# A third buffer for a rational MLP's polynomial, and a new order of work, behind gated linear attention

## The chip, the cores and the metric

The kernel runs on one core of a Trainium2 chip (trn2). The metric is device time in microseconds of one execution; kernels are compared by the median of several runs.

## What is computed

Gated linear attention over 4 batches of 8 heads, 768 tokens, head dimension 48, and behind it an MLP with a rational function in place of an activation. In the reference's words, cut:

```python
for t in range(S):
    state = alpha[:, :, t, :, None] * state + einsum('bhd,bhe->bhde', k[:, :, t], v[:, :, t])
    y[:, :, t] = einsum('bhd,bhde->bhe', q[:, :, t], state)
x = y.transpose(0, 2, 1, 3).reshape(3072, 384)
h = x @ w_in                               # 384 -> 2048
P = a[0] + a[1] * h + a[2] * h**2 + a[3] * h**3
Q = 1.0 + abs(b[0]) * abs(h) + abs(b[1]) * h**2
out = (P / (Q + 1e-06)) @ w_out            # 2048 -> 384
```

The inputs q, k, v and alpha are float32; the weights and coefficients come as float64.

## The kernel before

**Attention.** The sequence is cut in chunks of 128 tokens, and products of alpha are made with scans on VectorE (`suffix`, `prefix`), for 24 groups n of two chunks and four heads each. GpSimd multiplies k and q by them. 48 pieces i (a chunk and four heads) then go through TensorE (`sc_mm`), ScalarE (`sc_evac`), GpSimd (`sc_mask`, `decay`), TensorE again (`attn_mm`) and VectorE (`kv_add`). Two pieces make a chunk's output in PSUM bank 3, which ScalarE and VectorE split into a high and a low part (`x_hi`, `x_lo`), x for the MLP.

**Weights.** They come as pairs of 32-bit words of float64. Each of the 16 blocks (first layer i, second layer o, j = 0 to 7) is made float32 by one ScalarE step and three VectorE steps (`join_abs`, `join_sign`, `join_low`, `join`) and then split into a high part (ScalarE, `split_hi`) and a low part (`split_lo`; VectorE for j below 4, GpSimd from there).

**MLP.** There are 96 units u: 12 blocks of 256 tokens by 8 slices of 256 hidden columns. The first two token blocks are taken in two phases (slices 0 to 5, then 6 and 7), so that work can start before all weights are there. A unit's first layer (`mlp_in`, L562) is 18 products into PSUM bank u % 3; its second layer is 8 products with the high part gh (`mlp_out_hi`, L623) and 4 with the low part gl (`mlp_out_lo`, L633). Between them, on a 128 x 512 tile each:

- ScalarE: `act_t1` (L572) makes a2 + a3 h in tile t1; `act_ah` (L569) makes |h| in ah; `act_q1` (L575) makes b0 + b1 |h| in qm
- GpSimd: `pool_qm` (L578) multiplies qm by ah
- VectorE: `dve_t2`, `dve_t3` (L582, L586) go on with the polynomial in t1
- ScalarE: `act_ars`, `act_sq` (L589, L592) make a first reciprocal of Q in the PSUM bank
- VectorE: `dve_p`, `dve_t`, `dve_g` (L596, L599, L605) improve it and leave the quotient in t1
- ScalarE: `act_gh` (L608) makes gh from t1; GpSimd (VectorE for the first eight units): `sub_gl` (L612) makes gl from t1 and gh

So t1 holds the polynomial and then the quotient, and is free only when gl is done. t1, ah and qm have two buffers each, gh three, gl two. The bank is free for unit u + 3 when `dve_g` of unit u is done. The names in the profile leave buffer numbers out: t stands for t1.

**The verdict.** The fast attention is good for alpha within bounds. 18 loads of alpha and 36 ScalarE steps (`guard`, L663) count what is outside. After all other work `guard_verdict` sums this (VectorE, L672), adds over partitions (TensorE, L673, into bank 3) and compares with zero (VectorE, L675). Every engine then loads the result `ok` (L937) and branches on it (L938); a general path stands behind the branch, and does not run here.

**The order.** Every step is given to a `Plan` with its engine and the steps that it comes after. `Plan.run` issues the steps in the order of `ORDER`, a compressed list of numbers that was searched ahead of time. Each engine takes its own steps in that order, and waits on semaphores where a step needs another engine's result.

Of the kernel before, what the change touches and what calls it, by code (L numbers as in the profile page):

```python
# [12 lines left out]
F32 = mybir.dt.float32  # L13
# [9 lines left out]
class Plan:  # L23
# [35 lines left out]
    '6#q~Ml~o<b-;_vYQ(q{pnu5FO1d94gd+0n~!ka3mQu-gA#R~}fhDxVUUst5R(k+!<X?+p1tIOC=Wl-f*ke-TH(5T{y',
    'bwJ%!k@Q{?ZPgvMkG_#tMn6`;`a1=w`zo@w`UkyN<yDAw`kC_jfePpf>Ygg7DyoO7kgB8}sa&eC`k=z}b5%rrRG~Ut',  # L60
    '-&QZwQ&m|-(dY1+imIdOcj}F*ql&5@>WR96arGyaTgB5JqU%>Gy^f*d>+gz{R(VuRok4$933P<ctLm!Hs)S0Y>!~2f',
    'q)V!d`mM^W>#G1H)>(7|C6HAo(TTK!Z2F5TrIPAoT0=fnS|!&FRb+^zv+EQ(wyvryq||YA4qZkCLqXk2<<tzRbRk_$',
    'rPh%kjV`RKD+6hD5nV$S)#-Fq{ZiFb)$}h_OXboDpt>%uYwEa=TfbI~RSDf($A_P)n9ieH=n#kvC3Rk%PiKNZs+7Kp',
    'HFPX!qFU<wy0-qS;=nZ|D4_qT(z=$8fI9j*meKK`u5PMsVr!iN>S+ZTp}uaT(?bJYRs%HDJ#{(VOf}NIbYtCImDi(n',
    'Z~a@fP_6VBoe28swz`jQrxOA~1>Ik_*A;bQ7^?^9dss<#&`F@Rx{V!mKV4Z@(Vg@iY@*w!rh1_6tncD@-As4UZPi>o',
    'NO#rkR5v|XPtfD^JUv8rR1<Z3)m_imLv;_mP*2k9btp{Mi}WqLkHd6kND5Q*aNR>q)emtRmVlmWfgYi!=_mLIv%&_w',
    'SWnlFF$;{;8}$-BO3%<mp_f{!59<dwQ)h!^`iS1Fm+NBi5?AP1dW$})i^EDiTW`{<^c>w=9oK90R=ryHQET-!-B+#C',
    '$8;EM*C%xj*r8A9TyR2P)jM@|*rl)O(>fe-!gal$Zs-FP1<vT*IyyYXTl%ctqo3h9eOsT`&vBpLtCPcieL+WsWKb5~',
    '=offXmxcp68oa_Xa7cGj2X$xlRv)D4SOE@E4EU$t={vd<e9&FgYb+0U^+nxPDJ}_l;GPEVrt$)EBe<{M>&Eavzrlz4',
    'qrRk@L4S2wKhkfpDSXmb^kc1gfO?1JV4#Y|O&|qC=Y}vyHGmlWS*L_2da$YwsUSCe(W#*>5P#KmV2Jvr>%n*ZLq~90',  # L70
    'c&cA{;h*}sf2IxBhF|)*t_aEbg=X#yG5MALtz&aXNCTGt=s5gRJN~O<aTj>$J%7Lezt-s>E~ns55EI^G5dXlBm=AJt',
    'N{+<2_!Fk)$Q+M@IXB1W5KhAhI2DI-Le9&du@HoDB96je@i5K6w49j3xilZ4Zy1%+@psI_N%#w<=cJsU|6xAPz{$7(',
    'XXKxl9}03NE&_%4H)iGnP?)oD8UBMsI4fu4Us#qaL3S?Bf3Ya%;O<b4D{y6~%f+}GROC0lIM?G!+#4!$2`&g-p+2|g',
    'D%=B@8gNxE$%UaOG~{YrieLD~+=%-?2X4Z>Kv8vW%2l8SBX#7N*c@u|QF`l%YVk1|0ks*Z6KiS#!=Vm0;~LPF2Xbc~',
    '2hI7l@4|z)1&@SoEL0W7!eDO6wID#<xf-;DQP7Gfa}RFK6JRL!<TgAJdU0DG#zVL_x8u<;oTqRf9s?t|FR$WhJRU~!',
    'RPM*sVLE^C{dp3M;#pi1R`U!V&0}~bTUx`jc^wbnu{?*@v!Olgs4vXrz3gc&jN^G6O7ma>&*yzSo+t7GKEMkgh!*le',
    'UdxmCIL*QhyolfV`LLKz&_-Uu`?(b?<xL!!R`4Ni4a>M4tmMPIna}ZZ4yG-9o{#WW4xvbNl(%shMW+jVj61+~zQo5l',
    '3hm%FaDt=KP7bHb{D3cVKRC%(cnL(KUHsl(<%fKV7eRlx#=H3uFN3ylnjiBDxXx$z8ONa~e3ox;d-&`>`Ni;wZ}L-q',
    '&L919_{_KX1%LAcAO_v$mpmEna0Gqf+4zdL!Z&`+cX=QTfv>y;?(rLrML+mHf9HkpmIuL4W;sclAvXQuQzR0Tw!v?H',
    '$5Y@v8~MXK-~$f>D~aeYe`F`yAt2G^tN+Jdc0rIRi6J{-Dnt?xl$f#)NFvK%h$Xv0ON0bV3W+Uy;ENBDl(HA%$WZw1',  # L80
    'LnW2OrJp{v#FeEGCet83#gq7wU*b`?B%lNmMG{IvN+VGvk))Lr6iw1gVo4_jB!jGkq%s{cN)nj?ry-dXluS}lPC_Bc',
    'EVCfF6qYlPMJmZ}UsQ_7Daa~`sj?K4Igm|eLUBn-bFhSDm&THWl2J)HO--bfB&RBJhSE|FDJ@N9HsqA*QbwvuE~z19',
    'Wj}P4+>%!wK{aV6-K4p+lm}2wYDz0<A$g>{)ROy9L265Dc?c<~j<k`w(p~aNDrzhBWVrN{c2ZwfLuzUu?d1yek{;4f',
    'RzU}8Bp0E#q@iEFlk}1E&{0N6U%3D?rJt;UQF0kN%Sh=jYvCMpkqt0f2FNTq3qSlo86#t5kgS$VFk8mSU>PDRunxw{',
    'A3s#q!vq;7b7YN7lua;KHo_!HM{8xCOqTUBU((ZDoFWTkgY1>Fv{25`R5<|CWRYZ`>GBvB%M4j3OC%#bg?;kZZ<J@S',
    'N%l)7Iv`8s32c@ubO@Ho71<)0X}KJdt+GP0(l%KshvlGbmsPSuj>uKXMi@9MJ7t#~gln=}j>%Pc1&86f?2$Zl1ir#?',
    'c_z2y1RR4Kazb9fbNS~_%1!wWw<SBhkW+F;a?(+lhp*&0{E)kngI>#d`T_UkwEUF&l8au#8M#1b<(E8=Z*Wd>(@S{`',
    '=Y;|f<v6^NNEk4e<gHwgM-q&W<()i{KN1<A%5V8ALHJ(s(m&zAMfo6w=(6M|9r!591epTl0-pp-LCQyQ%xAd<Xuil-',
# [44 lines left out]
NNAT = 2  # L133
WB = 2
GB = 3
NSC = 2
TB = 2


@with_exitstack  # L140
def tile_gla_then_rational_mlp(ctx, tc, q, k, v, alpha, w_in, w_out, ca, cb, out):
    nc = tc.nc
    B, H, S, D = q.shape
    DM = H * D
# [381 lines left out]
    XB = 2  # L526
# [443 lines left out]
```

## Time and profile before

| | us |
|---|---|
| median of 3 runs | 604.32 |
| lowest and highest run | 602.88, 605.81 |
| the profiled execution, its own time | 600.71 |
| its span, first to last instruction | 599.0 |
| mean granted TensorE clock | 0.97 |

The span's rows are of one profiled execution. Busy time counts instructions that do work; loads of registers, branches and semaphores do not count. "PEld" is TensorE's loading of weights, which overlaps its products. A q behind an engine's name (SPq, PEldq) is its sequencer. An idle time is put down to the instruction that released the waiting one.

### The profile page before, as it was taken

To read this page: it belongs to the slowest core of one execution; us is meant where nothing else is said; L and a number is where in the kernel's file an instruction comes from. 1 tells how busy PE (TensorE), PEld (TensorE's weight loads), DVE (VectorE), ACT (ScalarE), POOL (GpSimd) and SP (SyncE) were. 2 spreads that over 40 slices of the span, in tenths; PEclk is the share of its full clock that TensorE was granted. 3 is DMA by queue.
4 is the path that set the end of the run, shared out by engine and by line. 5 is a ranking of instruction groups with operands and counts; after the bars stand their busy time and mean duration, and the time that the engine had idled before them with its cause. 6 is when DMAs were issued, how large, how long until landed. Compare 5 with 4: busy or idle time off the path is not lost. (4 is left out here: it accounts for less than half of the span.)

```text
span 599.0 us, 14096 instructions
## 1 busy us (share of the span) xinstructions
PE 540.2 (90%) x5362; PEld 503.4 (84%) x5362; DVE 503.8 (84%) x782; ACT 475.5 (79%) x803; POOL 400.3 (67%) x422
## 2 busy tenths in 40 slices
PE   4958359798789999999999999999999999999994
PEld 2647248697689999999999999999999999999993
DVE  4489999899979989989979889889889798778773
ACT  4478467687768799989898999998888787887972
POOL 6675453657687767687676777677766767565562
PEclk9998779799989999999999999999999999999999
DMA  9998542212442443414244344425230000000000
GB/s 170 248 367 275 94 55 32 30 28 34 56 94 58 72 80 72 64 28 69 61 68 89 49 92 79 76 47 76 30 44 26 14 27 2 2 27 1 27 1 32
DMA packets 179979, 41.90 MB, mean 70 GB/s; under 512 B 169409, under 2 KB 172481, under 8 KB 179905
## 3 DMA queue, kind: packets, MB, share of 16 engines
q1 hardware_dynamic: 179904, 40.94, 34.9%
q8 instruction: 44, 0.72, 0.5%
q14 instruction: 31, 0.25, 0.1%
HBM read 36.18 MB, written 4.72 MB: 68 GB/s over the span
## 5 line engine op out<-in xcount | busy, mean ns | idle before, releaser
L562 PE MATMUL ps<-x,wi 128*128 128x256 f32 x1728 | 232.7, 287 | 16.2 <-ACT wi L250 7.4
L562 PEld LDWEIGHTS ps<-x,wi 128*128 128x128 f32 x1728 | 220.9, 192 | 26.4 <-ACT wi L250 7.8
L623 PE MATMUL ps<-wo,gh 128*128 128x384 f32 x768 | 157.6, 344 | 16.2 <-DVE wo L257 6.7
L578 POOL TENSOR_TENSOR qm<-qm,ah 128x512 f32<-128x512 f32 x96 | 128.0, 1336 | 50.4 <-ACT qm L575 49.2
L612 POOL TENSOR_TENSOR gl<-t,gh 128x512 fp32r<-128x512 f32 x88 | 117.6, 1338 | 61.6 <-issue 30.3
L623 PEld LDWEIGHTS ps<-wo,gh 128*128 128x128 f32 x768 | 132.3, 190 | 21.3 <-DVE wo L257 6.9
L582 DVE TENSOR_TENSOR t<-t,ps 128x512 f32<-128x512 f32 x96 | 65.2, 680 | 33.6 <-ACT t L572 32.0
L633 PE MATMUL ps<-wo,gl 128*128 128x384 f32 x384 | 84.4, 342 | 0.3 <-POOL gl L612 0.3
L596 DVE SCALAR_TENSOR_TENSOR t<-t,coef,ps 128x512 f32<-128x512 f32 x96 | 71.0, 739 | 16.1 <-ACT ps L592 15.6
L575 ACT ACTIVATE qm<-ah,bab 128x512 f32<-128x512 f32 x96 | 77.8, 810 | 5.6 <-DVE ps L599 4.4
L589 ACT ACTIVATE ps<-qm,one_eps 128x512 f32<-128x512 f32 x96 | 66.1, 688 | 19.9 <-POOL qm L578 9.8
L572 ACT ACTIVATE t<-ps,coef 128x512 f32<-128x512 f32 x96 | 74.3, 774 | 7.3 <-POOL gl L612 4.3
L569 ACT ACTIVATE ah<-ps 128x512 f32<-128x512 f32 x96 | 56.9, 593 | 27.9 <-PE ps L562 26.5
L586 DVE SCALAR_TENSOR_TENSOR t<-t,coef,ps 128x512 f32<-128x512 f32 x96 | 71.4, 745 | 3.8 <-ACT ah L569 1.3
L608 ACT ACTIVATE gh<-t 128x512 fp32r<-128x512 f32 x96 | 60.1, 626 | 18.1 <-DVE t L605 16.0
L633 PEld LDWEIGHTS ps<-wo,gl 128*128 128x128 f32 x384 | 68.9, 191 | 1.4 <-POOL gl L612 0.9
L605 DVE SCALAR_TENSOR_TENSOR t<-ps,t 128x512 f32<-128x512 f32 x96 | 65.9, 687 | 2.1
L599 DVE SCALAR_TENSOR_TENSOR ps<-qm,ps 128x512 f32<-128x512 f32 x96 | 65.9, 687 | 0.0
L592 ACT ACTIVATE ps<-ps 128x512 f32<-128x512 f32 x96 | 56.1, 584 | 1.7
L444 PE MATMUL ps<-tq,tk 48*128 48x192 f32 (+1 forms) x384 | 46.1, 360 | 4.6 <-POOL tk L415 3.0
L457 POOL TENSOR_SCALAR_AFFINE_SELECT sc<-sc 128x512 f32<-128x512 f32 x48 | 31.9, 666 | 20.3 <-ACT sc L453 19.8
L453 ACT ACTIVATE sc<-ps 128x768 f32<-128x768 f32 (+1 forms) x48 | 37.0, 771 | 6.0 <-PE ps L444 3.6
(94 smaller groups left out, 603.9 us busy)
## 6 DMA issues: line engine op xcount, KB each, us to landing
wi_words<-in_moe_w_in_dram SPq DMA_DIRECT2D x8, 768.0 KB, 8.9
wo_words<-in_moe_w_out_dram SPq DMA_DIRECT2D x8, 768.0 KB, 10.3
tv<-in_v_dram SPq DMA_DIRECT2D x24, 192.0 KB, 3.2
wr<-in_alpha_dram SPq DMA_DIRECT2D x18, 256.0 KB, 2.9
out_dram<-parts SPq DMA_DIRECT2D x24, 192.0 KB, 2.0
raw_a<-in_alpha_dram SPq DMA_DIRECT2D x80, 32.0 KB, 2.1
raw_k<-in_k_dram SPq DMA_DIRECT2D x80, 32.0 KB, 2.1
raw_q<-in_q_dram SPq DMA_DIRECT2D x80, 32.0 KB, 2.1
```

Source lines behind the costliest of these rows:

```text
L562: nc.tensor.matmul(h_of(u)[:, ff * SEG : (ff + 1) * SEG], split_w["i", j][:, kt * FU + ff, w, :], x[:, kt, xp, :], start=(kt == 0 and n == ...
L572: nc.scalar.activation(buf(s, "t1", u), h_of(u), AF.Identity, bias=a2, scale=a3)
L575: nc.scalar.activation(buf(s, "qm", u), buf(s, "ah", u), AF.Identity, bias=b0, scale=b1)
L578: nc.gpsimd.tensor_tensor(buf(s, "qm", u), buf(s, "qm", u), buf(s, "ah", u), op=ALU.mult)
L586: nc.vector.scalar_tensor_tensor(t, t, a1, h_of(u), op0=ALU.add, op1=ALU.mult)
L589: nc.scalar.activation(h_of(u), buf(s, "qm", u), AF.Abs_reciprocal_sqrt, bias=one_eps)
L596: nc.vector.scalar_tensor_tensor(t, t, a0, h_of(u), op0=ALU.add, op1=ALU.mult)
L599: nc.vector.scalar_tensor_tensor(h_of(u), buf(s, "qm", u), 1.0 + 1e-6, h_of(u), op0=ALU.add, op1=ALU.mult)
L605: nc.vector.scalar_tensor_tensor(t, h_of(u), 2.0, t, op0=ALU.subtract, op1=ALU.mult)
L612: (nc.vector if GL_DVE[0] <= u < GL_DVE[1] and s is fast_bufs else nc.gpsimd).tensor_tensor(buf(s, "gl", u).rearrange("p a b -> p (a b)"), ...
L623: nc.tensor.matmul(o_of(tt), buf(s, "gh", u)[:, ff, tt * P : (tt + 1) * P], split_w["o", j][:, ff, w, :], start=(j == j0 and ff == 0 and w ...
L633: nc.tensor.matmul(o_of(tt), buf(s, "gl", u)[:, ff, tt * P : (tt + 1) * P], split_w["o", j][:, ff, 0, :], start=False, stop=(j == j1 and f ...
```

## The change

Three things change. The ring of t1 gets a third buffer (`TB`), so that `act_t1` of unit u waits for gl and gh of unit u - 3 in place of u - 2; the buffer counts of ah, qm and x get names, with the same values as before. The verdict's three instructions and its memset become steps of the plan. And `ORDER` is another list, so that steps of all engines stand elsewhere.

```diff
 ORDER = [
...
-    (the old list, 2846 steps)
+    (the new list, 2850 steps)
...
-TB = 2
+TB = 3
+QB = 2
+AB = 2
+NXB = 2
...
-    XB = 2
+    XB = NXB
...
-        "ah": ring("ah", 2, [P, N]), "t1": ring("t1", TB, [P, N]), "qm": ring("qm", 2, [P, N]),
+        "ah": ring("ah", AB, [P, N]), "t1": ring("t1", TB, [P, N]), "qm": ring("qm", QB, [P, N]),
...
-    def guard_verdict():
-        ones = const.tile([P, 1], F32, name="ones")
-        nc.gpsimd.memset(ones, 1.0)
-        tot = const.tile([P, 1], F32, name="tot")
-        nc.vector.tensor_reduce(tot, beyond, op=ALU.add, axis=mybir.AxisListType.X)
-        nc.tensor.matmul(ps[0:1, 3 * BANK : 3 * BANK + 1], tot, ones, start=True, stop=True)
-        ok = const.tile([1, 1], I32, name="ok")
+    vd_ones = const.tile([P, 1], F32, name="ones")
+    vd_tot = const.tile([P, 1], F32, name="tot_beyond")
+    ok = const.tile([1, 1], I32, name="ok")
+
+    def verdict_sum():
+        nc.vector.tensor_reduce(vd_tot, beyond, op=ALU.add, axis=mybir.AxisListType.X)
+
+    def verdict_mm():
+        nc.tensor.matmul(ps[0:1, 3 * BANK : 3 * BANK + 1], vd_tot, vd_ones, start=True, stop=True)
+
+    def verdict_ok():
         nc.vector.tensor_scalar(ok, ps[0:1, 3 * BANK : 3 * BANK + 1], 0.0, None, op0=ALU.is_equal)
-        return ok
...
-        add(("ah", u), "ACT", 0.6, act_ah, (u, fb), ins + [("qm", u - 2)])
+        add(("ah", u), "ACT", 0.6, act_ah, (u, fb), ins + [("qm", u - AB)])
...
-        add(("q1", u), "ACT", 0.82, act_q1, (u, fb), [("ah", u), ("t", u - 2), "bab"])
+        add(("q1", u), "ACT", 0.82, act_q1, (u, fb), [("ah", u), ("t", u - QB), "bab"])
...
+    add("vd_ones", "POOL", 0.1, nc.gpsimd.memset, (vd_ones, 1.0))
+    add("vd_sum", "DVE", 0.2, verdict_sum, (), [("gu", n, j) for n in range(NG) for j in range(2)])
+    add("vd_mm", "PE", 0.3, verdict_mm, (), ["vd_sum", "vd_ones", ("xl", 2 * NBLK - 1)], lat=0.13)
+    add("vd_ok", "DVE", 0.15, verdict_ok, (), ["vd_mm"], due=T0 + PACE * (NUA - 4))
...
-    ok = guard_verdict()
```

A list decodes with base85, zlib and 16-bit numbers; number n is the n-th step that the program adds to the plan. An engine's own order is what is left when the steps of the others are taken out. TensorE's last steps, as decoded ("in" a first layer, "out" a second layer, both by unit, "ol" the low part of a second layer; in 94 stands between the halves of out 90's high part):

```
before: in 89, in 90, out 86, out 87, in 91, in 92, out 88, out 89, in 93, in 94 (within out 90), out 90, out 91, in 95, out 92, out 93, out 94, out 95
after:  in 89, out 85, in 90, out 86, in 91, out 87, in 92, out 88, in 93, out 89, in 94 (within out 90), out 90, in 95, out 91, out 92, out 93, out 94, out 95
```

And VectorE around the verdict's steps and the last x_lo, as decoded:

```
after: ... p 82, t 82, g 82, x_lo 23, t2 83, ...    ... t2 87, t3 87, comparison of the verdict, p 86, t 86, ...
TensorE after: ... out 79, in 85, product of the verdict, out 80, out 81, ...
```

## Rows read from the trace of the kernel before

**Rows 1.** busy us and instructions by stretch: PE, PEld, DVE, ACT, POOL; clock; DMA; GB/s

```profile
0.00:36.00 36.00, 24.07 (x254) 17.95 (x255) 19.65 (x30) 17.49 (x37) 24.23 (x52) 1.00 1.14 230
...
36.00:165.00 129.00, 94.60 (x908) 84.85 (x906) 120.31 (x174) 90.92 (x138) 75.09 (x73) 0.88 0.45 97
...
200.00:540.00 340.00, 339.42 (x3553) 322.46 (x3552) 295.05 (x472) 298.79 (x517) 245.22 (x248) 1.00 0.29 52
...
540.00:593.00 53.00, 48.87 (x326) 46.86 (x324) 38.36 (x59) 41.35 (x69) 28.21 (x23) 1.00 0.02 9
```

**Rows 2.** waits, engine and line waited for: us, times, longest us, TensorE, whole span

```profile
PE ps L562 <- ACT wi L250: 7.4, 1, 7.4
...
PE ps L623 <- DVE wo L257: 6.7, 1, 6.7
```

**Rows 3.** timeline of the end: start, us, instruction, idle before it

```profile
578.05 0.68 DVE L605 SCALAR_TENSOR_TENSOR t<-ps,t 128x512 f32<-128x512 f32 x1
...
578.79 2.39 PE L562 MATMUL ps<-x,wi 128*128 128x256 f32 x18 [0.99 <-DVE t L605]
...
587.76 1.69 PE L623 MATMUL ps<-wo,gh 128*128 128x384 f32 x8 [2.34 <-ACT gh L608]
...
592.18 0.19 PE L673 MATMUL ps<-ones,tot 128*1 128x1 f32 x2
...
592.29 0.87 ACT L645 ACTIVATE parts<-ps 128x384 f32<-128x384 f32 x2 [2.54 <-PE ps L633]
```

**Rows 4.** chain that ended last, 515 to 540 us: start, us, what

```profile
524.91 4.26 PE ps L562 x36
...
529.17 1.39 PE ps L623 x8
...
533.86 0.70 PE ps L633 x4
```

**Rows 5.** groups by line, ScalarE's six: busy us, mean ns | idle before

```profile
L572 ACT ACTIVATE t<-ps,coef 128x512 f32<-128x512 f32 x96 | 74.3, 774 | 7.3 <-POOL gl L612 4.3 <-PE ps L562 2.3 <-DVE gl L612 0.3
...
L575 ACT ACTIVATE qm<-ah,bab 128x512 f32<-128x512 f32 x96 | 77.8, 810 | 5.6 <-DVE ps L599 4.4
...
L589 ACT ACTIVATE ps<-qm,one_eps 128x512 f32<-128x512 f32 x96 | 66.1, 688 | 19.9 <-POOL qm L578 9.8 <-DVE t L586 8.1 <-POOL tot L406 0.7
...
L608 ACT ACTIVATE gh<-t 128x512 fp32r<-128x512 f32 x96 | 60.1, 626 | 18.1 <-DVE t L605 16.0 <-DVE tot L672 1.4
...
L569 ACT ACTIVATE ah<-ps 128x512 f32<-128x512 f32 x96 | 56.9, 593 | 27.9 <-PE ps L562 26.5 <-DVE t L582 0.8
...
L592 ACT ACTIVATE ps<-ps 128x512 f32<-128x512 f32 x96 | 56.1, 584 | 1.7
```

**Rows 6.** instructions of L938 and L648 at the end, ns min/median/max

```profile
L938 ACTq COMPARE_BRANCH  x1: 50/50/50, 593.1 to 593.1; - x1
...
L938 PEldq COMPARE_BRANCH  x1: 3744/3744/3744, 593.2 to 593.2; - x1
...
L938 SPq EVENT_SEMAPHORE  x8: 17/17/17, 597.1 to 597.6; - x8
...
DMA to landing us min/median/max: 1.8/2.7/3.6
```

**Rows 7.** groups by line, four of VectorE's steps

```profile
L401 DVE TENSOR_TENSOR_SCAN fp<-ta,d 128x516 f32<-128x516 f32 x24 | 35.1, 1460 | 0.2
...
L537 DVE TENSOR_TENSOR x<-ps,x 128x384 fp32r<-128x384 f32 x24 | 13.1, 545 | 2.1 <-ACT x L532 2.1
...
L586 DVE SCALAR_TENSOR_TENSOR t<-t,coef,ps 128x512 f32<-128x512 f32 x96 | 71.4, 745 | 3.8 <-ACT ah L569 1.3
...
L380 DVE STREAM_TRANSPOSE tk<-raw_k 128x512 f32<-128x512 f32 x20 | 13.8, 691 | 0.0
```

**Rows 8.** instructions of L235 and L257 by form, ns min/median/max

```profile
L235 DVE SCALAR_TENSOR_TENSOR wi_words<-wi_words x8: 932/950/2020, 7.3 to 133.3; 128x768 uint32<-128x768 uint32 x8
...
L257 POOL TENSOR_TENSOR wi<-wr,wi x4: 1828/2200/3561, 66.9 to 139.1; 128x768 fp32r<-128x768 f32 x4
```

More of the change, by code (lines that the diff above doesn't have):

```diff
@@ L59 @@
[L59 to L88, printed above, removed]
@@ new lines @@
+    'U4?yA8{Vnc>KGlSG>{1L!x2gfIpHWJgO-pMl0$b$2Pq&Iq=%Hy2r|G=RRA(WaVQACR6oc9x#5q>3LW6L0==L9D%5Y(',
+    'LCOZ%;W)ilAJifGr^-PjeS)UYN3~m>p~#x_Cv}PTD5V9?(`OZ=E!+dGPf`?ZAez2F55WWLQ*@DTKy)3fPm|F%;fpE{',
+    'XG!#Z_^K+vJGe}R-~;ScS177JM|a_y+NZv&!Vp8>f*&eGSA^?O1f0$TURQ!UP!#gQBM8-%A%T7mF?E=J47VX4)PeNc',
+    'pw;0zgO1R3L1PI>r~|qlJb+9(u}-9`0^<|NsOy8r%(^5r0E<a<7VR*WPO7WHTZpYoK{6dz3qFI=5Kjj%xo!wkDTU6e',
+    'Q|jkXP`83N@B&^!DqTpY)>U<39Y+_{)gitvqO0jLPy^EF8al1cri<z7x+bL4we?fDLD_XJsG}oe4qaRaVNU%Ta_Pnp',
+    '2}|gjItn&{k~+7prAz6b&|Ei#x;h@V(Dn2mh>Ll2OPx>G*RLQx=GUcl9Q+Gq^i@(AfPYX{x7PRQ3pCI@bvfNeU!zaZ',
@@ new lines @@
+    'Q1{Y}bb0*|n!#w@M}LOAx;c!|fUR@^-CMWSEnuwfulwp>&`w{caIBy^!T?=SBevIJ7!@n&4mtu`!%eEJJL*VKMYn;k',
+    '&_p-ZKcJ~@3*&S%{T({#e!3k@)Zbvd?yTFxK%D?5>A8B44#q6lMbFcN^#t7mGT?9MrswOPkPy4;$$E$;oT3xqP`yz1',
+    'g7rEv4%1!r2Au?Z!vftyXU4^Pk?sSxX{yeI8+Biprti=QogQz|NWEE4*I99iKCEZxyA%zV>Wny3AJIv1na+jF^?iCm',
+    '$8-r?p@-|EdZm6y#qqd4ski8>`Vl>#oOnvF(vRty&W@XOCm5xR;td@guj^TQzsiQQ^#Qe7Z`E^j4&0{K=oolYzocRq',
+    'f=_9??hMmthkizP^a;IFKc}^NmyU_+^l80Y-_kEAIlj?*bSRd?Gy1KrfM@kyy-&Z>=X6=zuVdkReO@2X<?*h*p#SMZ',
+    '`jft`Kj>r#d{N)ipLIz@enkiMecc60A@OTUfnA{tzM<0iKz9Sh5A}39s2*v}Z|RV_q#tX;q1+!nYT=kX0KVvycv%mG',
@@ new lines @@
+    'uR0cA(XlZVrp9+P2)^mGI2gX`A@D=T;oO*<f9i@@7oX@9oEK|j9(<~qV{<cnrsMH*od)Zp<@lVEU+9MD_?P}bue9gR',
+    '_>q3=xE$a=Iu+N!_Y{f$>Q9t_({dNg$&vX7rQ=4Jnxk+o4&x>m&Ow}p^KeIu;Lnts^K&{(&rOj*LxR9pO2~ORA2!C)',
+    '{Ea%{VfBT|@OLV}i8uovQ4KI32Xk4@$Wgf-X5z$LkbhD%o<Zd~2EWw*C^MJi*ZMbA;O9OISLC`Jo&V4;3gN6=i3{;7',
+    'UymzuVg5@=xCl4kLYS0`a(zz5jky@-$I94{+jDU)fK|8&_r?zV!dK-++zYF5HtxiIupnmVrksO&Vl%GJg|P&8<mOz1',
+    '2XYJU%r&_y58~Ip8+YN7JcL_vDXxUAxCpYE%-wl7cgNP;gGcZb?tz23ClBRXTm`$~bgs=^u@?{HX<UbU^9%-6184C_',
+    'p3Qxj)J&SmM^$s2%58WQA5%(=#I{@uQB}n`yoyJ&R>QFx&gJUZj^FrExSC)3c^pt9uqMuDqt@_SzkomZzHHSPUdUtF',
@@ new lines @@
+    'seUYK53l8x=+!#jz>{z<M^)o^Bd_O)c#d1(K0d&$a5P3zn|K`d#e=+=qp0I*9&X{*c%FmQ2{oR_U}V*w+u#M>%E4*^',
+    '4&eQ~jW6*8UVw*q5kKJVe3-}LWxmJ{c|0EBD;!fz<fA-`u5vq^#PjhOU*pBx7U$x1Uc!%fDc|57e4L}H6}*hw<4Qik',
+    'k9j%AP&fG`cfecxgg@~qj;?O=GycpW>M8ffo&21a;#Uq;yZ8nF;N=)!?dF&KlfUo^jHT}IEB?l>IgUE1X47|m!^@CO',
+    'Toqdlz+Y_4Z=Q<r)LV{e{_q~OW*`p3L3o<~av~*WHx9-#?94tq%kTX^_U10{#ee~Gk3af%9Le10Q!27~&;1Zh6!U>6',
+    '<6?a0KXQ;6il6*KjAeq&5R7U*`xGX&S%fPwj+usJmS9|y(nK@y%}I=BQkeuQfk|z)U>XzMgsX2p%%nHla60BU;U<Hb',
+    'gAr;oMwkL7tx0GSs?(@UB2&nuGpA6S85pJtnxZC#NukbQMpMj$m`r9X&cuo)u_<gan<S=^$znoH5mVV@HC0SvRn^SK',
@@ L121 @@
+    'F}|Vi<OljWzL6i~=lQX|u^;T$__=<*U+X9M1%8O1=ok9Vev)70yZFg|vG3~F`zd~?pXxXHeSV#v<~REde!pMhH~OW1',
+    'm_Oi``QiSc-{LR$BYwF*>M#1OeuY2exB2P*vfu6x`x*X<-{EKatNyxQ>5utq{)S)WkNcf|wLjr+`dxmvKk0AzJ^qxx',
+    '?f3fA{*FKE&-lCkoWJMK`}_WZf9N0iOFplE>L2@O{)zt&MrO5h',
 ]
```

77 lines of the change are left out of this document (40 added, 37 removed).

## The prediction

> **What bounds the kernel now.** I read the busy time by stretch first, to see which engine is full where [rows 1]. From 200 to 540 us TensorE is busy 339.42 of 340 us, at a granted clock of 1.00, while VectorE stands at 295.05 and ScalarE at 298.79: this stretch is TensorE's, and an order or a buffer can win there only the 0.58 us that it stands idle. Before that it is another kernel: from 36 to 165 us VectorE is busy 120.31 of 129 us and TensorE only 94.60, at a clock of 0.88. The weights are being taken apart there, and the waits say that TensorE stands for them: 7.4 us for one first-layer weight, 6.7 us for one second-layer weight [rows 2]. At the end, from 540 to 593 us, TensorE loses again, 53 - 48.87 = 4.13 us [rows 1], and two waits name most of it: 2.34 us for gh and 0.99 us for the quotient [rows 3].
>
> Then I read the chain that ended last, for TensorE's price of one unit [rows 4]: 4.26 / 2 + 1.39 + 0.70 = 4.22 us. ScalarE's price of a unit is the sum of its six lines over 96 units [rows 5]: (74.3 + 77.8 + 66.1 + 60.1 + 56.9 + 56.1) / 96 = 4.08 us. So ScalarE is hardly below TensorE, which will matter at the end of this text.
>
> **The third buffer of t1.** It removes one dependency: the polynomial of unit u waits for gl and gh of unit u - 3 and no longer of u - 2. ah and qm keep two buffers (AB and QB are 2). Where the old dependency showed by itself, ScalarE stood 4.3 us ahead of L572 for it [rows 5], in an engine with 41 us to spare from 200 to 540: there I cost it at nothing, hidden behind TensorE, and without that cover it would be worth at most those 4.3 us. What the buffer does buy is room for the order. Decoding both lists of numbers (the section on the change says how), I counted the work of other units that stands on TensorE between the end of a unit's first layer and the start of its second layer, at 1.07 us for half a first layer and 0.70 us for a third of a second one (the attention left out). For units 16 to 89 its median was 10.4 us and becomes 16.3 us. In the full stretch this makes a late quotient less likely to stop TensorE; as it is stopped for 0.58 us only, I take 0, with -0.6 and +2 as bounds (a mark of 2 us would be one wait of the size in [rows 3]).
>
> **The tail.** In the last eight units the old order takes units in pairs: both first layers, then both second layers. The new one alternates: first layer of u + 4, second layer of u. With pairs, first layer u waits for the quotient of u - 3, which comes in bursts of two. The last instance can be read off: the quotient of unit 92 ends at 578.73 (578.05 + 0.68), TensorE starts unit 95 at 578.79 after standing 0.99 us, and stands another 2.34 us before 587.76, for gh of unit 94 [rows 3]. In the new order five units of second layers (5 x 2.09 = 10.5 us) stand behind the first layer of unit 95 in place of four (8.4 us), so there is work to cover the chain of units 94 and 95. The gain lies between 0 and the 3.5 us idle ahead of 592.3 (4.13 less 0.6 behind the last product); I take 2.5, nearer the upper end, since both waits named are of the kind that the alternating order spreads. What is late next is ScalarE: at 4.08 us of work for TensorE's 4.22 it leaves 0.14 us a unit, so I do not take all.
>
> **The verdict on alpha.** Before, its sum, product and comparison stood behind everything else. The sum on VectorE, the memset on GpSimd, the product on TensorE (0.19 us [rows 3]) and the comparison on VectorE, all of one column and small, now stand within the plan: GpSimd step 113 of 399, VectorE 602 and 703 of 750, TensorE 530 of 601. The product has a new wait, for the last x_lo (bank 3 is free then). Behind it on TensorE stands the second layer of unit 80, and everything after. On VectorE that x_lo stands right behind the quotient of unit 82, which TensorE needs for the first layer of unit 85 in any case, and that first layer, 2.13 us, stands ahead of the product: it covers the 0.55 us of x_lo [rows 7]. Without this cover the whole of TensorE would stand for it. Cost: 0.3 us, for the product itself and the break in the stream; bounds 0.2 and 2.5 (that wait, as long as the longest in [rows 3]).
>
> What it gives back is behind the last product. Every engine loads the verdict and branches on it; TensorE's branch took 3.744 us, from 593.2, so until 596.9; the last output landed 3.6 us after its issue at 593.2, where the other took 1.8; then SyncE's eight semaphores came at 597.1 [rows 6]. The output itself needs ScalarE's last copies, until 593.16 (592.29 + 0.87) [rows 3], so the verdict is not what holds the output. With the verdict known early the branch can start earlier; if the output then lands in 1.8 us, the end comes 1.8 us sooner; if the branch still starts behind the last product, nothing changes. Bounds 0 and -1.8; I take the middle, -0.9. The Trainium skill (Runtime: NRT & Kernel Launch, section Instruction fetch mechanics) says that a taken branch to a target that is not at hand has to wait until its page of instructions has been fetched. The trace agrees for TensorE (3.744 us) and not for ScalarE, whose branch took 0.050 us [rows 6]. By that rule the fetch stays, and only its place can move.
>
> **The start.** All queues are reordered here, SyncE's loads and GpSimd's set-up too, so a sum over moved steps would be noise. I use one cut instead: the moment when the last weight is joined, since behind it VectorE has less to do than TensorE. Ahead of that join the new order of VectorE has five more steps (a prefix scan, its reciprocal, one t2 and two t3) and two fewer (the transposes of k and q for one group): 1.46 + 3 x 0.745 - 2 x 0.69 = 2.3 us more, with t2 at t3's price and the reciprocal, of four columns, left out [rows 7]. Against it TensorE has one more first layer, that of unit 17, ahead of the second layer that waits for this weight: 2.13 us. The two cancel, to 0.2 us. What is left is whether VectorE stands idle more or less than now: 36 - 19.65 = 16.35 us up to 36 us and 129 - 120.31 = 8.69 us from there to 165 us [rows 1]. In favour: the new order puts nine more weight steps (among them the join and the low part of second-layer weight 1, and the low part of weight 0) ahead of the first quotient, where VectorE was waiting for the attention; and the low part of second-layer weight 2, for which TensorE stood 6.7 us, has 17 fewer steps ahead of it. Against: the first quotient itself comes later by 13 steps. I take -2, with -8.7 (all of the idle time after 36 us) and +10.7 (the slow rival) as ends.
>
> **Sum.** -2.5 - 0.9 + 0.3 + 0.2 - 2 + 0 = -4.9 us. On the profiled execution, 600.71 us (span 599.0, the rest lies around it), that is 595.8. This execution was 3.6 us quicker than the median of the three runs, 604.32; taken from the median, which is what will be compared, it is 599.4 us.
>
> **Rivals.** *No change:* TensorE is full for most of the span, the tail's waits only move from one instruction to another because ScalarE at 4.08 us a unit cannot follow, and the branch still starts behind the last product. Then -1 us is left of the tail and 0 of the rest: about 603.3. For it: the full stretch; against it: the four waits that the alternating order takes apart.
>
> *Slower, by VectorE held up in the start:* a step that joins weights usually takes 0.95 us, but has taken 2.02 us, and GpSimd's own low parts took from 1.83 to 3.56 us [rows 8]. So something holds one of the two while the other works. The new order starts GpSimd's products and low parts of the weights earlier, beside VectorE's densest stretch. There are 40 such steps on VectorE; if ten of them, a quarter, are held by the 1.07 us of the worst seen, the start is 10.7 us longer, and with the other terms (-2.5 - 0.9 + 0.3 + 0.2 = -2.9) the sum is +7.8: 612.1 us. It decides from three such steps on. Against it: now only a handful are stretched, their median, 0.95, is close to the minimum. The Trainium skill (SBUF — State Buffer, section Who interferes with whom) has a rule for it: a VectorE instruction with two inputs in SBUF and a GpSimd instruction that reads SBUF exclude one another, for the whole of an instruction. By that rule this rival is the one to come if GpSimd moves forward; the trace agrees that the stretched steps are of that kind.
>
> *A larger gain:* the start loses most of the idle 8.69 us, say 6.7 more than I hold: -11.6 us, 592.7.
>
> **How the numbers follow.** Forecast 0.50 (its own range 596 to 603), no change 0.19, slower 0.16, larger gain 0.15. A half per cent, 3 us, is what a measurement of this kernel can tell from none. So faster (below 601.3): 0.15 + most of 0.50, 0.57; within it: 0.19 and the upper edge of the forecast, 0.27; slower 0.16. The range reaches from behind the larger gain, 590, towards the slow rival, 608; what is outside is most of that rival and little below.
>
> **What would show it.** Right: TensorE's waits for gh and the quotient after 540 us add up to under 1.5 us; from the quotient of unit 92 to the last product 12.5 to 13 us in place of 13.5; the branch of TensorE done ahead of the last output's landing; the last join within 3 us of before. Wrong: VectorE's idle time from 36 to 165 us above 12 us, join steps with a mean well above 0.95 us, any TensorE wait above 1 us between 200 and 540 us, above all ahead of the verdict's product.

## The result, and the profile of the changed kernel

| | before | after |
|---|---|---|
| median, us | 604.14 (4 runs) | 596.90 (4 runs) |
| lowest to highest, us | 602.88 to 605.81 | 596.32 to 597.37 |
| profiled execution: its time, its span, us | 600.71, 599.0 | 596.56, 594.9 |

The ratio is 0.9878, interval 0.9852 to 0.9905; a second comparison, on another chip, gave 0.9866 (0.9844 to 0.9889). So the change makes the kernel 1.2% faster, 7.2 us by the medians, where 4.9 us were forecast. Line numbers of the changed kernel are higher by 3 (L562 is now L565, L605 is L608); the verdict's load and branch are now L947 and L948.

Busy time by stretch, columns as in [rows 1], after:

```profile
0.00:36.00 36.00, 22.34 (x240) 16.08 (x240) 16.24 (x26) 17.03 (x35) 18.62 (x50) 1.00 1.10 218
36.00:165.00 129.00, 97.55 (x918) 88.18 (x918) 122.69 (x176) 90.66 (x140) 69.72 (x73) 0.88 0.43 98
...
200.00:540.00 340.00, 338.69 (x3593) 321.85 (x3592) 293.49 (x474) 295.86 (x515) 243.17 (x247) 1.00 0.30 53
...
540.00:588.00 48.00, 47.48 (x322) 46.66 (x321) 36.64 (x55) 40.13 (x68) 28.25 (x22) 1.00 0.03 10
```

The stretch from 200 to 540 us is as full as it was. From 540 us to the last product TensorE is now busy 47.48 of 48 us; that is the large difference to [rows 1]. At the start VectorE is no less idle than before: 36 - 16.24 + 129 - 122.69 = 26.1 us, where [rows 1] give 16.35 + 8.69 = 25.0.

The timeline of the end after, as in [rows 3]: VectorE's quotient of unit 92, then what TensorE does behind it: the first layer of unit 95, the second layers of units 91 and 92, and (units 93 and 94 left out) that of unit 95:

```profile
573.78 0.69 DVE L608 SCALAR_TENSOR_TENSOR t<-ps,t 128x512 f32<-128x512 f32 x1
...
574.52 2.39 PE L565 MATMUL ps<-x,wi 128*128 128x256 f32 x18
576.75 1.55 PE L626 MATMUL ps<-wo,gh 128*128 128x384 f32 x8
578.14 0.86 PE L636 MATMUL ps<-wo,gl 128*128 128x384 f32 x4
578.83 1.55 PE L626 MATMUL ps<-wo,gh 128*128 128x384 f32 x8
580.22 0.86 PE L636 MATMUL ps<-wo,gl 128*128 128x384 f32 x4
...
585.23 1.55 PE L626 MATMUL ps<-wo,gh 128*128 128x384 f32 x8
586.62 0.86 PE L636 MATMUL ps<-wo,gl 128*128 128x384 f32 x4
```

No line of TensorE's there carries a bracket with an idle time; [rows 3] had 0.99 and 2.34 us there. From the end of that quotient, 574.47, to the last product's, 587.48, are 13.0 us, of which 2.13 + 5 x 2.09 = 12.6 are work.

To compare starts and tails of several kernels in one unit I use lost time: the time of a stretch less what the products that begin in it take in a full stream, where one follows the other without a stop (4.26 / 36 = 0.118 us for one of the first layer, 1.39 / 8 = 0.174 for one of the second [rows 4], and likewise for the attention's). It counts idle time and the lower clock together. One profiled execution each, us; "behind" runs from ScalarE's last copy to the end of the span:

```
                                   0-200   200-540   540-last product   last product at   behind
before, as shown                    77.4     2.3          5.0              592.25           5.85
before, a second profile            81.0     2.3          6.5              597.19           5.94
after, as shown                     77.7     1.7          0.6              587.48           6.47
after, a second profile             78.7     2.3          0.6              589.07           6.93
```

Two profiles of the same kernel differ, for before by 3.6 us in the start (the granted clock up to 36 us was 1.00 in the first and 0.91 in the second) and by 1.5 us in the tail, for after by 1.0 us in the start and 0.5 us behind the last copy. So the start's gain can't be read from this table; the tail's, 4.4 to 5.9 us, stands out; that the end became longer, by 0.5 to 1.1 us, does so only just.

### The profile page after: what moved, and what is told of

Read it like the earlier page. It is cut to its first block, busy times and chain, and to the rows that moved or that the text cites. A ratio compares the mean times of both kernels' runs of the same rounds, so it can differ in the third digit from the quotient of the medians.

```text
span 594.9 us, 14103 instructions
## 1 busy us (share of the span) xinstructions
PE 537.8 (90%) x5362; PEld 502.8 (85%) x5362; DVE 501.2 (84%) x782; ACT 472.8 (79%) x803; POOL 389.2 (65%) x422
## 4 chain that ended last, share of the span: by engine, by line
PE 72%; DVE 12%; SPq 5%; ACT 4%; DMA 4%; issue 2%; DVEq 0%; ACTq 0%
PE ps L565 31%; PE ps L626 19%; PE ps L636 10%; PE ps L490 6%; PE ps L447 5%; SPq L331 2%; SPq L356 2%; DMA wo_words<-in_moe_w_out_dram 2%; DVE wo_words L238 1%; DVE t L599 1%; DVE ps L602 1%; DMA wr<-in_alpha_dram 1%; DVE t L608 1%; DVE t L585 1%; PE ps L510 1%
## 5 line engine op out<-in xcount | busy, mean ns | idle before, releaser
L565 PE MATMUL ps<-x,wi 128*128 128x256 f32 x1728 | 231.3, 289 | 22.8 <-DVE t L608 10.7
L565 PEld LDWEIGHTS ps<-x,wi 128*128 128x128 f32 x1728 | 220.9, 195 | 32.0 <-DVE t L608 13.5
L599 DVE SCALAR_TENSOR_TENSOR t<-t,coef,ps 128x512 f32<-128x512 f32 x96 | 70.6, 737 | 18.7 <-ACT ps L595 18.2
L636 PE MATMUL ps<-wo,gl 128*128 128x384 f32 x384 | 83.1, 338 | 1.8 <-DVE gl L615 1.8
L572 ACT ACTIVATE ah<-ps 128x512 f32<-128x512 f32 x96 | 56.9, 594 | 15.7 <-PE ps L565 13.8
L608 DVE SCALAR_TENSOR_TENSOR t<-ps,t 128x512 f32<-128x512 f32 x96 | 65.9, 687 | 2.3
L447 PE MATMUL ps<-tq,tk 48*128 48x192 f32 (+1 forms) x384 | 44.3, 349 | 1.1 <-POOL tq L422 1.1
L460 POOL TENSOR_SCALAR_AFFINE_SELECT sc<-sc 128x512 f32<-128x512 f32 x48 | 33.4, 697 | 18.0 <-ACT sc L456 17.8
```

The lines of the kernel that those rows point to most:

```text
L447: nc.tensor.matmul(bank(home(i) + j)[:, SW * a : SW * a + w], tk[n % NQ][r, c, :], tq[n % NQ][r, c, 0:w], start=True, stop=True,)
L565: nc.tensor.matmul(h_of(u)[:, ff * SEG : (ff + 1) * SEG], split_w["i", j][:, kt * FU + ff, w, :], x[:, kt, xp, :], start=(kt == 0 and n == ...
L599: nc.vector.scalar_tensor_tensor(t, t, a0, h_of(u), op0=ALU.add, op1=ALU.mult)
L608: nc.vector.scalar_tensor_tensor(t, h_of(u), 2.0, t, op0=ALU.subtract, op1=ALU.mult)
L636: nc.tensor.matmul(o_of(tt), buf(s, "gl", u)[:, ff, tt * P : (tt + 1) * P], split_w["o", j][:, ff, 0, :], start=False, stop=(j == j1 and f ...
```

## Experiments on the order and the buffer

**The kernel before, once more**, as a base for the scatter.

> The kernel before, unchanged, profiled once more: its profiled execution took 600.71 us where its timed runs took 604.14, while the changed kernel's profiled execution, 596.56, agrees with its runs (596.9). Ratio 1.000 +- 0.002 in either case. If the profiled execution shown was just a quick one, this profile comes near 604 and its rows show 3 us more of TensorE's idle time in one stretch; theory A (the tail holds all of the gain) expects those 3 us at the end, behind 540 us; theory B (the start holds a part) expects them before 200 us.

605.01 us, ratio 1.0007 (0.9992 to 1.0022). So the method shows differences from some 0.2% up. Its profile is the second line of the table: its execution took 5.0 us longer than the one shown first, 3.6 us of it before 200 us (theory B) and 1.5 us behind 540 us (theory A).

**The buffer alone**, old order.

```diff
-TB = 2
+TB = 3
```

> The order before with three buffers for t1 (TB = 3) and nothing else. Theory A and the prediction: the buffer is room for the order only, so 0 (ratio 0.997 to 1.003); the 4.3 us that ScalarE stood for gl lie beside TensorE's work. Rival: the waits for gl do hold the tail's chain, then -1 to -2 us (0.997 to 0.998), and the idle time of ScalarE's t1 behind gl falls from 4.3 us to 0 in both cases.

603.48 us, ratio 0.9995 (0.9976 to 1.0014): nothing that shows, and by the interval a gain of 1.5 us at most. Its row for the polynomial on ScalarE shows that the edit took effect and is worth nothing:

```profile
L572 ACT ACTIVATE t<-ps,coef 128x512 f32<-128x512 f32 x96 | 73.9, 771 | 2.7 <-PE ps L562 2.7
```

The 4.3 us of waiting for gl in [rows 5] are gone, and the time stays the same: that wait was covered, as the prediction had it. The rival, 1 to 2 us, is excluded only for its larger half.

**Each half of the order by itself**, both with three buffers. The lists are cut behind the last piece of the attention on TensorE (`attn_mm` of piece 47), which ends at 533 us before and 524 us after; so the head holds the start and most of the full stretch too. One kernel takes the old list up to there and the new one behind it, with the verdict in the plan:

```diff
+        cut = old.index(keys.index(("am", 47))) + 1
+        head = old[:cut]
+        order = head + [n for n in new if n not in set(head)]
```

> Three buffers; all engines in the old order up to the last attention product, then what is left in the new order, the verdict in the plan. Theory A (the tail holds the gain): -4 us, ratio 0.992 to 0.995, TensorE idle under 1 us from 540 us to its last product. Theory B (start and middle hold at least half): -1 us or none, ratio 0.997 to 1.000.

The other takes the new list up to there and the old one behind it, with the verdict last:

```diff
+        cut = new.index(keys.index(("am", 47))) + 1
+        head = new[:cut]
+        order = head + [n for n in old if n not in set(head)] + verdict
```

> The counterpart: three buffers; the new order up to the last attention product, then what is left in the old order, with the verdict's product and comparison last. Theory A: within 1 us of before if the start is even, at most -3 us if the timed runs' extra 3 us belong to the start (ratio 0.995 to 1.001), and TensorE again idle about 3 us behind 540 us. Theory B: -4 to -7 us (0.988 to 0.993).

The new tail alone: 600.84 us, ratio 0.9950 (0.9934 to 0.9967). The new head alone: 601.39 us, ratio 0.9962 (0.9943 to 0.9980). The first lies at the edge of what theory A gave (0.992 to 0.995), the second within theory A's range (0.995 to 1.001); but A's leading thought, that the tail holds all of it, does not stand. Each has about half of the gain, and their product, 0.9912, is near the 0.9866 to 0.9878 of the whole, whose intervals it overlaps when its own are multiplied (0.988 to 0.995). The stretch from 540 us in the one and in the other, columns as in [rows 1]:

```profile
540.00:593.00 53.00, 50.85 (x344) 49.78 (x344) 40.32 (x60) 43.12 (x71) 30.79 (x24) 1.00 0.03 10
```

```profile
540.00:593.00 53.00, 49.01 (x325) 46.63 (x323) 38.73 (x59) 41.77 (x70) 28.79 (x23) 1.00 0.03 9
```

With the new tail (first row, last product at 591.55) lost time behind 540 us is 1.5 us; with the old tail it is 5.2 us, as in the kernel before. The new head has 77.6 us lost up to 200 us, the old one with three buffers 78.7 and 78.9: the right sign, but less than two profiles of one kernel differ by. What the new head is worth is shown by the times alone.

What the new head does is seen in TensorE's waits from 36 to 200 us, old order with three buffers first, then after (us in total, times, longest):

```profile
PE ps L623 <- DVE wo L257: 8.3, 1, 8.3
PE ps L562 <- ACT wi L250: 7.4, 1, 7.4
PE ps L623 <- POOL wo L257: 4.3, 2, 2.8
...
PE ps L562 <- DVE t L605: 3.7, 2, 3.4
```

```profile
PE ps L565 <- DVE t L608: 10.1, 5, 4.8
PE ps L565 <- ACT wi L253: 7.8, 2, 7.7
PE ps L626 <- ACT gh L611: 5.1, 1, 5.1
...
PE ps L626 <- POOL wo L260: 2.4, 2, 1.5
...
PE ps L636 <- DVE gl L615: 1.8, 2, 1.1
PE ps L626 <- DVE wo L260: 0.9, 1, 0.9
```

The second-layer weights' 8.3 + 4.3 us shrink to 0.9 + 2.4. In their place TensorE waits for quotients, gh and gl, 17.0 us in place of some 4. Most of the wait only changed its name: VectorE makes the quotients and joins the weights. All lines of the two views together, those left out here too, give 37.4 us with the old order and 35.9 us after.

**The new order with two buffers.** In the new list 75 of the 94 polynomials from unit 2 on stand ahead of the gl that two buffers would make them wait for; in the old list none does. So the new list can't be run with two buffers as it is. I mended it in two ways. In the first, a step that comes too early is put off until what it waits for is placed:

```diff
-TB = 3
+TB = 2
+        while todo:
+            for n in todo:
+                if all(a in placed for a in after(n)):
+                    break
+            todo.remove(n)
+            order.append(n)
+            placed.add(n)
```

> The changed kernel with two buffers for t1. In the new list a step that would come before one it waits for is put off until that one is placed; the rest of the order stays. Theory A (the alternating tail and the start win by the order, the buffer only makes such orders possible): the polynomial of unit u waits for gl of u - 2 again, waits of ScalarE for gl return, and TensorE's waits for the quotient and gh after 540 us come back in part; 1 to 4 us slower than the changed kernel, ratio to before 0.990 to 0.996. Rival B (the buffer is needed at every unit, since more work of other units stands between a first and its second layer): TensorE stops all through 200 to 540 us, over 6 us slower than the changed kernel, ratio about 1 or above. Rival C (the buffer does nothing even in the new order): ratio 0.988.

In the second, the steps that it waits for are pulled forward instead:

```diff
-TB = 3
+TB = 2
+        def place(n):
+            if n not in placed:
+                for a in after(n):
+                    place(a)
+                placed.add(n)
+                order.append(n)
+        for n in given:
+            place(n)
```

> The changed kernel with two buffers for t1, and the new list mended in the other way than before: ahead of a step stand the steps that it waits for, pulled forward, so that the quotient and gl of u - 2 come ahead of the polynomial of u. In the new list 75 of the 94 polynomials stand ahead of the gl that two buffers make them wait for, in the old list none. Theory A (order and buffer only work together): the pulled steps stand on VectorE, ScalarE and GpSimd ahead of work that is needed sooner, TensorE's waits for the quotient and gh come back over the whole stretch from 200 to 540 us, slower than the kernel before, by more than 3 us and less than the mending by putting off. Rival B (the mending by putting off was a bad order, and the third buffer is worth little): within 3 us of the changed kernel.

799.91 and 801.02 us, ratios 1.3219 (1.3186 to 1.3252) and 1.3234 (1.3197 to 1.3271). I expected the first 1 to 4 us above the changed kernel; it was 203 us above it, which was the rival's side, and far beyond it. The second I expected above the kernel before and below the first; it was above, by some 196 us, but not quicker than the first. ScalarE's first wait in the second, and TensorE's:

```profile
ACT t L588 <- POOL gl L628: 143.0, 75, 5.9
```

```profile
PE ps L578 <- DVE t L621: 84.1, 41, 4.2
```

The polynomial waits for gl of two units before, 143 us in all, and the quotients that TensorE needs come late. The traces give a simple account. A buffer of t1 is held from the start of `act_t1` to the end of gl. For units 20 to 88 the median of that time is 9.97 us before, 13.55 after and, with two buffers, 14.0 in the first mended order and 14.2 in the pulled one. A unit comes every 5.25 us there before (attention included), 5.26 after. Two buffers held 9.97 us allow one unit in 5.0 us, which is enough; held 14.0 or 14.2 us they allow one in 7.0 or 7.1 us, and 7.43 and 7.38 were measured; three held 13.55 us allow one in 4.5. So the old order needed no third buffer, and the new one, as mended here, can't do without it. The granted clock may count as well: in these two kernels it was 0.91 to 0.93 from 200 to 600 us, where the changed kernel had 1.00 from 200 to 540 us; how much of the 200 us that makes was not separated. These two mended orders were not searched; they show what this order costs with two buffers, not the best that two buffers allow.

## Experiments on the end of the program

Before these runs I formed a theory of why the early verdict brought nothing. The verdict's load and branch after, ns, then where:

```profile
L947 SPq TENSOR_LOAD <-ok x1: 503/503/503, 589.4 to 589.4; - x1
...
L948 SPq EVENT_SEMAPHORE  x8: 17/17/17, 593.0 to 593.5; - x8
...
L948 PEldq COMPARE_BRANCH  x1: 3427/3427/3427, 587.0 to 587.0; - x1
...
L948 ACTq COMPARE_BRANCH  x1: 50/50/50, 588.0 to 588.0; - x1
...
L948 SPq COMPARE_BRANCH  x1: 45/45/45, 590.2 to 590.2; - x1
```

TensorE's branch does come earlier, and is done at 590.4, ahead of the last output's landing. But SyncE has the last output to issue (588.5 to 589.3), and takes its load and branch behind that, at 589.4 and 590.2; then its next instruction comes at 593.0, 2.7 us later. Before, the same gap was 2.5 us, from its branch to the semaphores at 597.1 [rows 6]:

```profile
L938 SPq COMPARE_BRANCH  x1: 45/45/45, 594.5 to 594.5; - x1
```

If that sets the end, it does not matter when the verdict is known.

**The verdict last again**, all else as after:

```diff
+        late = [the four vd_ steps]
+        order = [n for n in order if n not in late] + late
```

> The changed kernel with the verdict's sum, product, comparison and memset put behind everything else, as in the kernel before; buffer and order stay. Theory A (SyncE's own load of the verdict and its branch stand behind the issue of the last output, so they end the program whenever the verdict is known): within 0.7 us of the changed kernel, ratio to the kernel before about 0.988. Rival B (my prediction's, an early verdict brings 0.9 us): 0.9 us slower than the changed kernel, ratio about 0.9895, and the span behind ScalarE's last copies grows. Rival C (the early verdict costs, because the end behind the last copies was 0.6 us longer in the changed kernel): faster by 0.6 us.

596.14 us, ratio 0.9853 (0.9829 to 0.9877), 6.29 us behind the last copy. That is 0.8 and 0.6 us below the changed kernel in its two comparisons, at other times. So rival B is out: the early verdict brings no 0.9 us. Theory A and rival C, by which it costs 0.6 us, are not told apart by these times.

The traces say more. In all eleven profiles here of a kernel that branches and issues its last output from SyncE, the end behind the last copy is 2.92 to 2.95 us plus two times of SyncE: its issue of the last output, and the gap from its branch to its next instruction. That is 0.38 + 2.54 us before, 0.38 + 2.63 in the second profile, 0.84 + 2.69 after, 1.33 + 2.65 in its second profile, and 0.38 + 2.98 with the verdict last. The rest is the same to 0.03 us, so neither TensorE's branch nor the landing of the output adds to it, before as little as after. Where the verdict is early the issue is longer, 0.77 to 1.33 us in five of six profiles, for 0.38 in all five with the verdict last; the gap goes from 2.43 to 2.69 us with an early verdict and from 2.54 to 3.04 with a late one. What lengthens either was not tried. The last two issues together, before and after:

```profile
592.80 0.81 SPq L648 DMA_DIRECT2D out_dram<-parts  x2
```

```profile
588.03 1.27 SPq L651 DMA_DIRECT2D out_dram<-parts  x2
```

**The last block's output from ScalarE's queue**:

```diff
-        nc.sync.dma_start(rows, buf(s, "part", 2 * m + tt))
+        eng = nc.scalar if m == NBLK - 1 else nc.sync
+        eng.dma_start(rows, buf(s, "part", 2 * m + tt))
```

> The changed kernel with the stores of the last token block issued from ScalarE's queue in place of SyncE's. Theory A (SyncE's load of the verdict and its branch, behind the issue of the last output, set the end): SyncE branches ahead of the last copies, and the end comes 1.5 to 2.5 us sooner than in the changed kernel, ratio to before 0.984 to 0.986; the end behind ScalarE's last copies falls from 6.5 us to between 4 and 5. Rival B (the landing of the last output sets the end): within 0.5 us of the changed kernel, ratio about 0.988.

594.89 us, ratio 0.9836 (0.9812 to 0.9861; I gave 0.984 to 0.986), 4.33 us behind the last copy in place of 6.3 to 6.9. Its rows (lines are one higher):

```profile
L949 SPq EVENT_SEMAPHORE  x8: 17/17/17, 565.8 to 590.9; - x8
L949 SPq COMPARE_BRANCH  x1: 45/45/45, 563.3 to 563.3; - x1
...
L949 PEldq COMPARE_BRANCH  x1: 3644/3644/3644, 586.5 to 586.5; - x1
```

SyncE now branches at 563.3, its first semaphore comes at 565.8, again 2.5 us later, and both lie beside the last units. That is the direct test of the theory, and it holds. What ends this kernel is then the landing of the last output, at 590.58: SyncE's next semaphore comes at 590.59. This kernel is the quickest here that does all the work; against the kernel with the verdict last, on the same chip, the medians differ by 1.25 us.

**No branch.** This kernel leaves out the load of the verdict, the branch and the general path, so what is done for alpha beyond its bounds:

```diff
-    fine = nc.values_load(ok[0:1, 0:1], min_val=0, max_val=1)
-    with tc.If(fine == 0):
-        general()
```

> The changed kernel without the load of the verdict, the branch and the general path behind it; it leaves out the reaction to alpha beyond its bounds. Theory A (SyncE's load, branch and what it fetches behind the branch stand at the end): the end behind ScalarE's last copies falls from 6.5 us to about 4, ratio to before about 0.984. Rival B (the landing of the last output sets the end): within 0.5 us of the changed kernel.

592.78 us, ratio 0.9808 (0.9783 to 0.9834), 3.06 us behind the last copy, so below the 0.984 and the 4 us that I gave. A part of it is the landing. From the DMA view from 580 us, queues that carried something and the output's median time to landing, after first, then without the branch:

```profile
q1 hardware_dynamic: 288, 0.39, 7.2%
q14 instruction: 6, 0.05, 1.1%
q8 instruction: 2, 0.03, 0.8%
...
out_dram<-parts SPq DMA_DIRECT2D x2, 192.0 KB, 2.4
```

```profile
q1 hardware_dynamic: 288, 0.39, 8.8%
...
out_dram<-parts SPq DMA_DIRECT2D x2, 192.0 KB, 1.9
```

Without the branch no instructions are fetched at the end, and the output lands in 1.9 us in place of 2.4. So the branch costs the program some 3.4 us behind the last copy (6.47 - 3.06): the last output lands 2.60 us behind that copy in place of 1.96, which is 0.6, and the other 2.8 lie between that landing and the end. The other queue gives back 2.1 of the 3.4.

## An experiment on the start

**Eight low parts of gl moved from VectorE to GpSimd**, in the same places of the order, with the changed kernel beside it on the same chip.

```diff
-GL_DVE = (0, 8)
+GL_DVE = (0, 0)
```

> The changed kernel as it is, on the same chip as the next two, as their base. Both theories: ratio to the kernel before 0.985 to 0.990.

> The changed kernel with the low parts gl of the first eight units made on GpSimd in place of VectorE, in the same places of the order: VectorE has 8 x 0.70 = 5.6 us less to do before 170 us, GpSimd 8 x 1.31 = 10.5 us more. Theory A (from 36 to 165 us VectorE sets the time, whatever TensorE is named to wait for): the last join comes 3 to 5.6 us sooner and the kernel is 2 to 5 us faster than the changed kernel. Rival B (GpSimd or the clock sets it as well, or the two hold each other up): the last join moves by less than 1.5 us, VectorE's idle time from 36 to 165 us grows by most of the 5.6 us, and the time is within 1 us or longer.

The changed kernel: 596.77 us, ratio 0.9866 (0.9844 to 0.9889). With less on VectorE: 601.41 us, ratio 0.9946 (0.9924 to 0.9967), so 4.6 us slower, where I expected 2 to 5 us faster. The last join came at 169.75, not at 166.77. The stretch from 36 to 165 us, changed kernel first, then with the eight steps moved:

```profile
36.00:165.00 129.00, 95.62 (x877) 86.56 (x878) 122.49 (x175) 90.43 (x139) 68.96 (x72) 0.87 0.43 98
```

```profile
36.00:165.00 129.00, 93.45 (x860) 84.97 (x861) 122.08 (x162) 88.14 (x136) 82.72 (x78) 0.86 0.43 97
```

VectorE does 13 instructions fewer and is busy just as long, 122.08 us for 122.49. So it isn't idle more, as the rival had it; its steps have become longer. One place of the timeline of this kernel, GpSimd's gl and product, and two of VectorE's join steps:

```profile
132.78 1.28 POOL L615 TENSOR_TENSOR gl<-t,gh 128x512 fp32r<-128x512 f32 x1
...
133.02 1.86 DVE L238 SCALAR_TENSOR_TENSOR wi_words<-wi_words 128x768 uint32<-128x768 uint32 x1
...
134.93 1.30 POOL L581 TENSOR_TENSOR qm<-qm,ah 128x512 f32<-128x512 f32 x1 [0.86 <-ACT qm L578]
134.99 2.06 DVE L244 SCALAR_TENSOR_TENSOR wr<-wr,wi_words 128x768 uint32<-128x768 uint32 x1
```

GpSimd's instructions end at 134.06 and 136.23; VectorE's end 0.82 and 0.82 us behind them. A join step alone takes 0.95 us [rows 8], so it looks as if VectorE stood until GpSimd was done and then did its work. In this kernel 23 of VectorE's steps before 172 us are longer by over 0.15 us than the shortest of their form, each of them beside a GpSimd instruction, by 18.2 us in all; 8 of them, with 6.6 us, beside one of the gl on GpSimd. In the changed kernel there are 18, with 12.1 us. Steps that take one input from PSUM are not stretched: `dve_t3` and `dve_p` have a mean of 0.732 us in this kernel and 0.731 in the changed one. The Trainium skill (SBUF — State Buffer, section Who interferes with whom) says that a VectorE instruction with two inputs in SBUF excludes a GpSimd instruction that reads SBUF, for the length of an instruction. The trace agrees, with these 0.82 us. That sentence does not cover all that is held: 4 of the 23 steps, with 2.8 us, have one input in SBUF and constants, such as the `join_sign` that took 2.14 us at 86.11, for 0.55, beside a GpSimd step. So VectorE's 5.6 us were given back as held-up time, which accounts for no loss and no gain. The loss of 4.6 us is not shown by that. GpSimd, with 13.8 us more of busy time in that stretch, is late for others: TensorE waits 4.0 us for gl there from 36 to 200 us, where it waited 2.1 us in the changed kernel. The granted clock, 0.86 for 0.87, may have a part too; neither was tried by itself.

## Why the prediction was right or wrong

The sign and the time were right (596.9 in the range from 590 to 608 around 599.4). That the sum came so near is in part luck: the term for the end missed by 1.4 to 2.0 us one way, that for the tail by 1.9 to 3.4 us the other. The terms, one by one:

- **The buffer, 0.** Right: 0.9995 alone. What I gave as its use, room for the order, is what the runs with two buffers show; I had not seen how much hangs on it. The work counted between a unit's layers, 10.4 and 16.3 us, was the right sign of it.
- **The tail, -2.5 (bounds 0 and -3.5).** Right mechanism, mis-sized: the waits for gh and the quotient are gone altogether (under 1.5 us was asked for), and lost time behind 540 us falls by 4.4 in the shown profiles, by 5.9 in the second ones. The bound was wrong too: it counted TensorE's idle time alone, 3.5 us, where the same execution has 5.0 us of lost time, and it was read from one execution that was quicker than the median; another lost 6.5. And ScalarE, at 4.08 us a unit to TensorE's 4.22, did keep up; holding 1 us back for it was unfounded.
- **The dense stretch, 0.** Right: 338.69 of 340 us busy; lost time 1.7 and 2.3 us for 2.3 in both of before.
- **The verdict's instructions, +0.3.** Too small to be seen; their wait for the last x_lo was covered as said.
- **The end of the program, -0.9 (0 to -1.8).** The step that failed. TensorE's branch did finish ahead of the last landing, as forecast, and the last output landed 2.5 us behind the start of its issue in place of 3.6; but I took the wrong thing for the limit. SyncE's own load, its branch and the 2.5 us until its next instruction, which I had not read in the trace of before, stand behind its issue of the last output in any case. The end behind the last copy became 0.5 to 1.1 us longer in place of shorter, nearly all of it in that issue, 0.84 and 1.33 us for 0.38; why the issue is longer stays open.
- **The start, +0.2 - 2.** About the right size (the new head alone is worth 0.38%, 2.3 us) but not by the step I gave, so that the size is luck. VectorE's idle time fell from 36 to 165 us (6.31 for 8.69), as hoped, but rose as much and more up to 36 us (19.76 for 16.35), 26.1 for 25.0 in all, and the last join did not come sooner (165.72 for 162.59, and 165.33 in the second profile of before; the two shown are below). The second-layer weights for which TensorE stood do come in time, as said, but the quotients come later instead. Which part of the rearranged waits is the 2.3 us was not taken apart.

```profile
161.65 0.94 DVE L241 SCALAR_TENSOR_TENSOR wr<-wr,wo_words 128x768 uint32<-128x768 uint32 x1
```

```profile
164.78 0.93 DVE L244 SCALAR_TENSOR_TENSOR wr<-wr,wo_words 128x768 uint32<-128x768 uint32 x1
```

- **The signs named ahead.** From the quotient of unit 92 to the last product 13.0 us (12.5 to 13 asked for); VectorE idle 6.31 us from 36 to 165 us (under 12); no TensorE wait above 0.5 us between 200 and 540 us; the last join 3.1 us later where 3 was the limit, by the shown profile of before, and 0.4 by the second.
- **The slow rival.** It did not come: the join steps that took 0.95 us still do in the median, and 16 of VectorE's steps before 172 us are held, by 10.4 us in all, where before 16 were held by 10.2:

```profile
L238 DVE SCALAR_TENSOR_TENSOR wi_words<-wi_words x8: 943/948/1852, 7.3 to 129.4; 128x768 uint32<-128x768 uint32 x8
L238 DVE SCALAR_TENSOR_TENSOR wo_words<-wo_words x8: 941/971/2047, 32.2 to 162.5; 128x768 uint32<-128x768 uint32 x8
```

The holding-up is real, though: eight more GpSimd steps in that stretch, and VectorE was busy as long with 5.6 us less to do. The prediction said that the stretched steps are of the kind with two inputs in SBUF; of the 16 before, 4 have one input there, with 3.1 of the 10.2 us.

The gain by the medians, 7.2 us, is larger than what the spans of the profiles show (594.9 and 596.9 for 599.0 and 604.0, a mean of 5.6); with before's profiles 5 us apart, that difference can't be placed in a stretch.

## What to carry to other kernels

Count how long a buffer is held, not only who waits for it: buffers divided by hold time is the rate that they allow, and an order that interleaves more units pays for it in buffers, so the two have to be changed together. At the end of a program, follow each engine's own last instructions in its own order; an engine that issues the last transfer and then branches puts its branch behind that issue, and another queue for the transfer took it off the path here (2.1 us behind the last copy). Work moved from VectorE to GpSimd need not free VectorE: here 5.6 us of it came back as steps held up beside GpSimd's.

## What was not expected of the hardware

- In the traces here SyncE's branch is recorded with 45 ns, and its next instruction comes 2.4 to 3.0 us later; TensorE's is recorded with 3.4 to 4.2 us; ScalarE's, some 50 ns, is followed within 0.5 us. Idle time of this kind is not named in the chain of waits.
- In the twelve profiles with a branch the last output landed 2.3 to 4.1 us behind the start of its issue; without the branch, and without instructions fetched, it took 1.9. That the fetch is the cause is likely, but not shown.
- Two VectorE join steps that began under a GpSimd instruction ended 0.82 us behind it, so almost their whole 0.95 us was still to do.
